# A three-stage kernel on Trainium2: another weight conversion, one form for all experts' second layers, and new planner tables

## The chip, the cores and the metric

The kernel runs on one core of a Trainium2 chip. The metric is the device time of one execution in microseconds, as the median of several runs. Before the change it is 784.63 us (three runs, 784.27 to 784.72).

## What is computed

Three stages, each feeding the next: attention with a hashed mask, a dense two-layer network, and eight experts with a greedy assignment of tokens. All inputs are fp32, except that the network's weights `w_in` and `w_out` come as 64-bit words, of which the kernel reads a high and a low half.

```python
def _attn_ref(q, k, v, proj):            # (2, 8, 768, 64)
    q_bits = (einsum('bhsd,dk->bhsk', q, proj) > 0)    # k likewise
    q_bucket = sum(q_bits * powers)                    # 6 bits
    scores = where(q_bucket == k_bucket, q @ k.T / sqrt(D), -1e9)
    attn = exp(scores - max); attn = attn / (sum(attn) + 1e-9)
    return attn @ v                                    # -> x: 1536 x 512
def _moe_ref(x, w_in, w_out):            # 512 x 2048, 2048 x 512
    h = maximum(x @ w_in, 0)
    return h * h @ w_out
def _moe2_ref(x, w_gate, w1, w2):        # 8 experts, 512 x 1024, 1024 x 512
    order = argsort(-(x @ w_gate).flatten())
    # greedy: each token goes to the first expert in this order that has room (192)
    for e in range(8):
        out[assigned == e] = maximum(x[assigned == e] @ w1[e], 0) @ w2[e]
```

## The kernel before

The program is one core's work on five engines, written in an order that a planner makes. `Sched` holds the operations of each stage: engine, planned duration, what they need, a priority, which buffers they take (`acq`) and give back (`rel`). `order` runs a list schedule with these durations and writes the instructions out in the order that results; `port=True` marks VectorE steps that the planner doesn't let run beside GpSimd's. The tables `PR` (attention), `MP` (network), `EP` and `RP` (router) and `FP` (experts) are priorities by kind of operation. On the chip each engine then works through its own instructions in this order and waits at semaphores; the planner's times decide nothing else.

Attention (0 to about 260 us): 96 blocks of 128 rows. TensorE makes scores (L582), VectorE their maximum (L598), ScalarE the exponential (L601), GpSimd scales (L610), TensorE transposes (L618), ScalarE and VectorE copy the transposes in two parts (L626, L630), TensorE multiplies with the values (L639, L640).

Network (about 240 to 525 us): the weights come in 16 chunks `f`, each an in- and an out-part of 128x512 words. `conv` (L804 to 818) makes fp32 of the two halves: step 0 on ScalarE takes the absolute value of the high half, steps 1 to 4 on VectorE are L812, L814, L816 and L818. `raw` holds the two halves, `t` the word that is put together, `x` the result. Later steps split into fp32r parts (L822, L887, L909), TensorE transposes (L878, L902) and multiplies (L926), and L943 evicts.

Router and experts (525 to 782 us): the router assigns tokens in rounds, on VectorE above all; L1606 are long steps of a round (44 of them, 600 to 1012 ns), L1613 the small matmuls beside them. Each round's end gives the row numbers `ix` of the next expert (L1736). GpSimd fetches these rows by two indirect transfers (L1911), TensorE transposes them (L1929, L1931), and the expert `p` begins: first layer L1967 in four groups `g` of fp32 matmuls, then the second layer. `HP = 2`: experts 0 and 1 take `add2`, the others `add2r`.

- `add2`: after a zeroing matmul (L2014), fp32 matmuls (L2008) give the transposed output, relu'd by ScalarE or VectorE (L1971); it is evicted (L2067 ScalarE, L2069 VectorE), transposed back (L2076), copied (L2083, L2085).
- `add2r`: the second layer's weights are split in two fp32r parts (L1885 ScalarE, L1887 VectorE), the relu'd hidden layer too (L1978 ScalarE, L1981 VectorE, two pieces), and fp32r matmuls of 512 columns give the output itself (L2036, L2037, L2038 for tokens 0 to 127; L2040, L2043 for the rest), evicted at L2099, L2101, L2103.

Then GpSimd scatters the output rows (L2089, L2090), two scatters per expert. All work on GpSimd is in one queue, so a scatter that waits keeps the next gather waiting.

Of the kernel before, what the change touches and what calls it, by code (L numbers as in the profile page):

```python
# [81 lines left out]
class Sched:  # L82
# [24 lines left out]
    def order(self):  # L107
# [51 lines left out]
        while left:  # L159
# [34 lines left out]
            if locks:  # L194
                port = t + dur
# [526 lines left out]
LEAST = 3.4332275390625e-05  # L722
MP = {"lw": -774.5, "ac": 24.5, "h1": -252.5, "h2": 273.5, "ch": -3545, "hw": 253.5, "we": -1093, "wn": -1773, "cv": -742, "sp": -3335.5, "sm": -1005, "xs": -292.5, "sq": -2724, "lg": -93.5, "ev": 307.5, "lv": 292, "c0": 8976.5, "c1": 6037.5, "b0": 230.5, "b1": 3618}


def mlp(nc, S, ps, mem, ident, xhi, xlo, w_in, w_out, w_gate, wgt, x2d, L, att):
# [391 lines left out]
    def last_logits(n, s, rel):  # L1118
# [10 lines left out]
        for h in range(2):  # L1129
            T["lt", n, h] = a = S.add("PE", .22, lambda h=h: half(n, h, 1), [(e, f)[h], a], prio=q, acq=("B",) if h else ("B", "xt"))  # L1130
# [6 lines left out]
    def out(n, s):  # L1137
# [8 lines left out]
        T["lt", n] = a = S.add("PE", .44, lambda: logit(n, 0), [e], prio=p(s, "lg"), acq=["B", "xt"])  # L1146
# [35 lines left out]
    for f in range(16):  # L1182
# [3 lines left out]
        dur = (.61, 1.135, 1.135, 1.14)  # L1186
# [670 lines left out]
def experts(tc, nc, S, ps, mem, ident, router, x2d, w1, w2, out, L, cst, slot):  # L1857
# [43 lines left out]
    def before(p):  # L1901
# [316 lines left out]
```

## Time and profile before

| | |
|---|---|
| median of three runs | 784.63 us |
| profiled execution: its own time | 783.99 us |
| span of its records | 782.2 us |
| TensorE (PE) busy | 755.5 us, 97% |
| VectorE (DVE) busy | 588.1 us, 75% |
| ScalarE (ACT) busy | 462.3 us, 59% |
| GpSimd (POOL) busy | 341.6 us, 44% |

The busy times are sums over instructions on each engine; an fp32 matmul stands in the trace as two records. PEclk is the clock that TensorE was granted, as a share of full speed. Idle time is shown with the instruction that ended it and what it waited for ("<-").

### The profile page before, as it was taken

Reading aid. Unit: us, or ns where it says so; the run is one execution under the profiler, and the core shown is the slowest. Engines: PE = TensorE matmul, PEld = TensorE weight load, DVE = VectorE, ACT = ScalarE, POOL = GpSimd, SP = SyncE. Lnnn points to the kernel's source line nnn. Section 1 sums busy time; section 2 is a strip of 40 time slices with the busy share of each in tenths; the row PEclk is TensorE's granted clock in tenths of the full one; section 3 lists DMA queues with packets and bytes.
Section 4 is the critical chain, followed back from the end, with each engine's and each line's share of the span. In section 5 each row is a group of like instructions: output and inputs, shape, how many; then the busy total and the mean of one; then the engine's idle time right before and its main releaser. Section 6 shows DMA issues by size and latency. Waiting matters only on the chain.

```text
span 782.2 us, 14059 instructions
## 1 busy us (share of the span) xinstructions
PE 755.5 (97%) x4979; PEld 663.1 (85%) x4979; DVE 588.1 (75%) x1243; ACT 462.3 (59%) x949; POOL 341.6 (44%) x376
## 2 busy tenths in 40 slices
PE   8899999999999999999999999999999799999996
PEld 6689888898887889998888989898589698888885
DVE  6789999999999896599979775438877577753432
ACT  7889889889898665553666665455503212333332
POOL 3578788787797776555410000009320412231111
PEclk9999999999999999999999999999799899999999
DMA  8979658575721122310311310201176475897000
GB/s 173 236 139 182 146 108 187 123 136 129 170 60 56 54 74 89 108 54 0 109 54 54 108 55 1 81 27 55 60 252 203 144 259 191 284 340 257 21 12 29
DMA packets 77732, 94.33 MB, mean 121 GB/s; under 512 B 29632, under 2 KB 56640, under 8 KB 77664
## 3 DMA queue, kind: packets, MB, share of 16 engines
q1 hardware_dynamic: 75616, 87.16, 41.1%
q0 software_dynamic: 2048, 6.29, 2.6%
q8 instruction: 39, 0.64, 0.3%
q14 instruction: 29, 0.24, 0.1%
HBM read 63.55 MB, written 6.29 MB: 89 GB/s over the span
## 4 chain that ended last, share of the span: by engine, by line
PE 64%; DVE 17%; issue 9%; ACT 5%; DMA 2%; POOL 1%; SPq 0%; POOLq 0%; ACTq 0%; DVEq 0%
PE psS L926 9%; PE psS L1967 7%; PE psS L582 5%; DVE p L630 4%; PE psTP L902 4%; PE psm L902 4%; DVE f L598 4%; PE psTP L878 3%; PE psO L926 3%; PE psS L2008 2%; PE psTP L926 2%; PE psm L878 2%; DVE tz L865 2%; PE psTP L618 2%; PE psO L1339 1%
## 5 line engine op out<-in xcount | busy, mean ns | idle before, releaser
L610 POOL TENSOR_TENSOR f<-f 128x768 f32<-128x768 f32 x96 | 141.9, 1480 | 30.9 <-PE psTP L618 8.2
L926 PE MATMUL psS<-r 128*128 128x512 f32 x384 | 100.6, 395 | 0.3 <-DVE f L943 0.3
L824 POOL TENSOR_TENSOR r<-f,r 128x384 fp32r<-128x384 f32 (+3 forms) x58 | 74.8, 1312 | 55.6 <-ACT r L822 52.4
L598 DVE TENSOR_REDUCE f<-psS 128x1 f32<-128x768 f32 x96 | 90.7, 946 | 3.6 <-PE psS L582 3.4
L582 PE MATMUL psS<-r 128*128 128x384 f32 x384 | 88.7, 352 | 4.2 <-DMA r<-r 1.8
L601 ACT ACTIVATE f<-psS,f 128x768 f32<-128x768 f32 x96 | 88.1, 917 | 3.4 <-DVE f L598 2.1
L926 PEld LDWEIGHTS psS<-r 128*128 128x128 f32 x384 | 70.5, 188 | 13.6 <-DVE f L943 1.1
L1967 PE MATMUL psS<-ff,rf 128*128 128x192 f32 x400 | 77.8, 338 | 0.0
L582 PEld LDWEIGHTS psS<-r 128*128 128x128 f32 x384 | 64.2, 188 | 10.1 <-ACT f L601 7.1
L822 ACT ACTIVATE r<-f 128x384 fp32r<-128x384 f32 (+3 forms) x112 | 56.4, 533 | 27.7 <-DVE f L818 11.7
L2090 POOL DMA_INDIRECT out_dram<-ff,ix x16 | 22.2, 1385 | 112.1 <-DVE ff L2101 67.2
L1967 PEld LDWEIGHTS psS<-ff,rf 128*128 128x128 f32 x400 | 66.7, 195 | 1.6 <-DVE ff L1938 0.3
L1475 POOL TENSOR_SCALAR f<-f,mx 128x768 bf16<-128x768 f32 (+1 forms) x3 | 8.3, 2755 | 134.5 <-ACT f L1461 134.5
L630 DVE TENSOR_TENSOR p<-psTP,p 128x384 fp32r<-128x384 f32 x93 | 49.8, 548 | 6.4 <-ACT p L626 6.0
L626 ACT ACTIVATE p<-psTP 128x384 fp32r<-128x384 f32 x93 | 45.3, 503 | 8.8 <-PE psTP L618 8.3
L1887 DVE TENSOR_TENSOR ff<-rf,ff 128x1024 fp32r<-128x1024 f32 x22 | 26.9, 1222 | 31.4 <-ACT ff L1885 31.4
L1885 ACT ACTIVATE ff<-rf 128x1024 fp32r<-128x1024 f32 x22 | 23.3, 1058 | 44.6 <-PE psS L2038 36.3
L1911 POOL DMA_INDIRECT ff<-x2d,ix x16 | 19.5, 1218 | 68.8 <-DVE cq L1803 28.8
L618 PE MATMUL psTP<-ident,f 128*128 128x128 f32 x279 | 46.3, 275 | 0.5 <-DVE p L630 0.4
L824 DVE TENSOR_TENSOR r<-f,r 128x384 fp32r<-128x384 f32 (+3 forms) x54 | 30.5, 582 | 18.0 <-ACT r L822 17.9
L913 ACT ACTIVATE f<-f 128x384 f32<-128x384 f32 x63 | 31.9, 521 | 16.2 <-DVE f L909 15.2
L618 PEld LDWEIGHTS psTP<-ident,f 128*128 128x128 f32 x279 | 34.3, 140 | 7.5 <-DVE p L630 2.0
(448 smaller groups left out, 1950.7 us busy)
## 6 DMA issues: line engine op xcount, KB each, us to landing
rf<-in_moe_w_dram SPq DMA_DIRECT2D x60, 512.0 KB, 6.8
r<-r SPq DMA_DIRECT2D x90, 192.0 KB, 4.3
f<-in_moe_w_in_dram SPq DMA_DIRECT2D x16, 512.0 KB, 3.8
f<-in_moe_w_out_dram SPq DMA_DIRECT2D x16, 512.0 KB, 4.7
r<-r SPq DMA_DIRECT2D x15, 384.0 KB, 3.9
f<-in_q_dram SPq DMA_DIRECT2D x8, 384.0 KB, 6.4
f<-in_k_dram SPq DMA_DIRECT2D x8, 384.0 KB, 7.8
f<-in_v_dram SPq DMA_DIRECT2D x8, 384.0 KB, 5.9
```

Of the source, the lines that this page charges most:

```text
L582: nc.tensor.matmul(sbank(u)[:, hf, 0:384], T["q", (pr, h)][:, n, 128 * i:128 * i + 128], T["k", (pr, h)][:, n, 384 * hf:384 * hf + 384], s ...
L598: nc.vector.tensor_reduce(col(0, u), sbank(u)[:, :, 0:384], axis=AX.XY, op=OP.max, negate=True)
L601: nc.scalar.activation(P(u).rearrange("p (a b) -> p a b", a=2), sbank(u)[:, :, 0:384], AF.Exp, bias=col(0, u), accum_out=col(1, u))
L610: nc.gpsimd.tensor_tensor(Pn(u), P(u), col(3, u).to_broadcast([128, 768]), op=OP.mult)
L618: nc.tensor.transpose(tp(u, g)[:, j], Pn(u)[:, 128 * c:128 * c + 128], ident)
L626: nc.scalar.activation(th, tp(u, g), AF.Copy)
L630: nc.vector.tensor_tensor(tl, tp(u, g), th.bitcast(F32), op=OP.subtract)
L822: nc.scalar.activation(hi, x, AF.Copy)
L824: (e or nc.gpsimd).tensor_tensor(lo, x, hi.bitcast(F32), op=OP.subtract)
L902: nc.tensor.matmul(wbank(s, k), w[x][:, c], y[z][:, c], start=st and c == i == 0, stop=c == 1 and i == 2, skip_group_check=not st)
L926: nc.tensor.matmul(abank(i), a[:, t], w, start=(f == RUNS[r][1][0] and j == 0), stop=(f == RUNS[r][1][-1] and j == 2))
L1967: nc.tensor.matmul(abank(n)[:, j], raw(p, g)[:, 0, 256 * c + 128 * j:256 * c + 128 * j + 128], xT(p)[:, c], start=(c == 0), stop=(c == 3))
```

## The change

It has four parts.

- `conv`: ScalarE's absolute value now goes to `t`; a maximum of `t` with the constant `LEAST` (L812, one tensor, in place) replaces the comparison; shift and mask move to L814; the two combining steps stay (L816, L818) and the last writes `x`. The step that multiplied with the comparison's result is gone. Step count stays four on VectorE. `LEAST` gets another value, and the raw buffer is given back with step 4, not 3.
- `HP = 0`: experts 0 and 1 take `add2r` like the others. Buffers `yT` and `hx` go, `wh` gets three places in place of two, `hr` four in place of three, and the raw tiles become 15 in place of 16.
- The planner's durations of GpSimd's transfers (gather 3.6 and 2.1 to 3.8 and 2.7, scatter 1.1 to 1.4) and a weight for the logits' transposes are other numbers; `port` of a VectorE step is tested a little differently.
- All priority tables have new numbers.

From L2033 on, line numbers of the kernel after are two higher.

```diff
-PREP, PW, DL = -40.5, 0.8, 2.4
-PREP1 = 3
+PREP, PW, DL = -38, 0.8, 2.4
+PREP1 = 10
-PR = {"S": 22, "mx": 1264, "ex": -144, ...
+PR = {"S": 21.5, "mx": 2686.5, "ex": 33, ...
-LEAST = 3.4332275390625e-05
+LEAST = 3.0517578125e-05
         if j == 0:
-            nc.scalar.activation(x, hw.bitcast(F32), AF.Abs)
+            nc.scalar.activation(t.bitcast(F32), hw.bitcast(F32), AF.Abs)
         elif j == 1:
-            V.tensor_scalar(t, hw, 3, 0x3FFFFFF8, op0=OP.logical_shift_left, op1=OP.bitwise_and)
+            V.tensor_scalar(t.bitcast(F32), t.bitcast(F32), LEAST, None, op0=OP.max)
         elif j == 2:
+            V.tensor_scalar(t, t, 3, 0x3FFFFFF8, op0=OP.logical_shift_left, op1=OP.bitwise_and)
+        elif j == 3:
             V.scalar_tensor_tensor(t, hw, -0x40000000, t, op0=OP.bitwise_and, op1=OP.bitwise_or)
-        elif j == 3:
-            V.scalar_tensor_tensor(t, lw, 29, t, op0=OP.logical_shift_right, op1=OP.bitwise_or)
         else:
-            V.scalar_tensor_tensor(x, x, LEAST, t.bitcast(F32), op0=OP.is_ge, op1=OP.mult)
+            V.scalar_tensor_tensor(x.bitcast(I32), lw, 29, t, op0=OP.logical_shift_right, op1=OP.bitwise_or)
...
-        dur = (.61, 1.135, 1.135, 1.14)
+        dur = (.61, .61, 1.135, 1.135)
...
-HP = 2
+HP = 0
-RF = (8,) * 11 + (3, 3, 3, 1.5, 1.5)
+RF = (8,) * 11 + (3, 3, 3, 3)
-UNITS_F = {"raw": ..., "wh": (5008, 5016), "yT": (5024, 5027), "yl": (5056,), "hx": (4097, 4098.5, 5030), "hr": (4088, 4091, 4094),
+UNITS_F = {"raw": ..., "wh": (5008, 5016, 5024), "yl": (5056,), "hr": (4088, 4091, 4094, 4097),
...
-        T["ga", p] = ga = S.add("POOL", 2.1 if p else 3.6, gather, [ids], prio=FP["ga"], acq="xg")
+        T["ga", p] = ga = S.add("POOL", 2.7 if p else 3.8, gather, [ids], prio=FP["ga"], acq="xg")
...
+            if (p, g, j, b) == (0, 0, 0, 1):
+                ps.part(unit(("y", p), "S"))
...
-            T["sc"] = a = S.add("POOL", 1.1, lambda h=h: scat(h), [e, T.get("sc")], prio=FP["sc"])
+            T["sc"] = a = S.add("POOL", 1.4, lambda h=h: scat(h), [e, T.get("sc")], prio=FP["sc"])
```

GpSimd's order around the fetch of expert 2, before. `ix_5618` are the row numbers of expert 0, `ix_5961` of expert 1, `ix_6320` of expert 2.

```order
L1911 DMA ff9_5412<-x2d_82,ix_5961 128x512
L1911 DMA ff9_5412<-x2d_82,ix_5961 64x512
L1916 COPY ei_5846<-ei_5846 128x1
L2089 MEMSET pad_93 128x1
L2090 DMA out_0_dram<-ff12_5415,ix_5618 1536x512
L1911 DMA ff8_5411<-x2d_82,ix_6320 128x512
L1911 DMA ff8_5411<-x2d_82,ix_6320 64x512
```

The same place after; the row numbers are `ix_5612`, `ix_5974` and, of expert 2, `ix_6417`.

```order
L1911 DMA ff8_5407<-x2d_82,ix_5974 128x512
L1911 DMA ff8_5407<-x2d_82,ix_5974 64x512
L1916 COPY ei_5842<-ei_5842 128x1
L2091 MEMSET pad_93 128x1
L2092 DMA out_0_dram<-ff11_5410,ix_5612 1536x512
L2091 MEMSET pad_93 128x1
L2092 DMA out_0_dram<-ff12_5411,ix_5612 1536x512
L1911 DMA ff7_5406<-x2d_82,ix_6417 128x512
L1911 DMA ff7_5406<-x2d_82,ix_6417 64x512
```

Before, one scatter of expert 0 stands ahead of the gather of expert 2 and the other behind it; after, both stand ahead.

VectorE around the row numbers of expert 2, before.

```order
L1606 TENSOR_SCALAR ff19_5422<-ff18_5421,mx_6208 128x1152
L2085 COPY ff12_5415<-psO_63 64x512
L1736 CAST ix_6320<-psTP0_60 128x2
L1606 TENSOR_SCALAR ff20_5423<-ff18_5421,mx_6208 128x1152
L1606 TENSOR_SCALAR ff21_5424<-ff18_5421,mx_6208 128x1152
L1606 TENSOR_SCALAR ff22_5425<-ff18_5421,mx_6208 128x1152
L1887 TENSOR_TENSOR ff2_5405<-rf8_5392,ff1_5404 128x1024
```

The same place after.

```order
L1981 SCALAR_TENSOR_TENSOR rf13_5394<-psS10_5435,rf13_5394 128x2x64
L1981 SCALAR_TENSOR_TENSOR rf13_5394<-psS10_5435,rf13_5394 128x2x128
L1718 TENSOR_TENSOR mv_6358<-h_6339,tok1_100 128x9
L1726 TENSOR_TENSOR ff25_5424<-ff30_5429,pk_6349 128x1152
L1720 TENSOR_TENSOR mv_6358<-tok1_100,mv_6358 128x9
L1562 TENSOR_TENSOR Bb_6365<-w_6288,alive1_99 128x72
L1606 TENSOR_SCALAR ff20_5419<-ff17_5416,mx_6270 128x1152
L1564 TENSOR_SCALAR PM_6387<-Bb_6365 128x72
L1606 TENSOR_SCALAR ff21_5420<-ff17_5416,mx_6270 128x1152
L1736 CAST ix_6417<-psm_62 128x2
L1565 TENSOR_TENSOR PM_6387<-PM_6387,mx_6270 128x72
L1887 TENSOR_TENSOR ff6_5405<-rf8_5389,ff5_5404 128x1024
```

The copy of expert 0's output (L2085), whose scatter GpSimd's next row is, stood right ahead of the row numbers; now the steps of the hidden layer's second part (L1981) stand there, and the copy's successor stands 44 rows earlier. After `ix_6417` and the L1887 four L1606 follow in a row; before, seven with an L1887 between them.

## Rows read from the trace of the kernel before

**Rows 1.** Windows: stretch, its length, busy us (and instructions) of each engine, PEclk
```profile
45.00:231.00 186.00, 183.92 (x1199) 163.63 (x1197) 173.94 (x357) 171.57 (x389) 148.29 (x168) 1.00 0.66 139
231.00:395.00 164.00, 157.66 (x825) 140.69 (x826) 140.90 (x197) 96.74 (x197) 102.96 (x91) 1.00 0.20 65
...
565.00:640.00 75.00, 70.89 (x742) 63.95 (x740) 52.19 (x179) 17.39 (x27) 18.25 (x17) 0.94 0.61 202
...
620.00:640.00 20.00, 20.00 (x145) 18.62 (x145) 13.06 (x59) 2.98 (x6) 2.68 (x4) 0.86 0.77 254
```

**Rows 2.** Groups by line and form: engine, operation, shapes, count | busy us, mean ns
```profile
L818 DVE SCALAR_TENSOR_TENSOR f<-f 128x1024 f32<-128x1024 f32 x16 | 21.9, 1370 | 0.3
...
L812 DVE TENSOR_SCALAR f<-f 128x1024 int32<-128x1024 int32 x16 | 12.9, 808 | 1.8 <-DMA f<-in_moe_w_out_dram 1.8
L1606 DVE TENSOR_SCALAR ff<-ff,mx 128x1152 bf16<-128x1152 f32 x16 | 12.2, 811 | 0.7 <-ACT ff L1580 0.7
```

**Rows 3.** Timeline of TensorE, 231 to 395 us, rows with idle time in brackets
```profile
231.05 0.97 PE L582 MATMUL psS<-r 128*128 128x384 f32 x4 [0.32 <-ACT f L601]
...
380.38 1.31 PE L902 MATMUL psTP<-f,r 128*128 128x384 f32 x6 [1.29 <-DVE f L909]
...
394.46 0.72 PE L926 MATMUL psS<-r 128*128 128x512 f32 x2 [0.34 <-DVE f L943]
```

**Rows 4.** Groups by line and form, experts' stage
```profile
L1887 DVE TENSOR_TENSOR ff<-rf,ff 128x1024 fp32r<-128x1024 f32 x22 | 26.9, 1222 | 31.4 <-ACT ff L1885 31.4
...
L2090 POOL DMA_INDIRECT out_dram<-ff,ix x16 | 22.2, 1385 | 112.1 <-DVE ff L2101 67.2 <-DVE ix L1736 22.7 <-DVE m L1560 9.4
...
L1981 DVE SCALAR_TENSOR_TENSOR rf<-psS,rf 128x256 fp32r<-128x256 f32 x18 | 7.4, 414 | 0.0
```

**Rows 5.** Timeline of TensorE, experts: start us, duration us, instruction
```profile
610.56 2.76 PE L2008 MATMUL psS<-rf,rf 128*128 128x192 f32 x16
613.15 1.05 PE L1613 MATMUL psTP<-Bb,ff 128*128 128x8 bf16 x36
...
618.18 0.44 PE L1929 MATMUL psO<-ident,ff 128*128 128x128 f32 x2 [3.55 <-DMA ff<-x2d,ix]
619.18 0.47 PE L1931 MATMUL psO<-ident,ff 64*128 64x64 f32 x2 [0.56 <-DMA ff<-x2d,ix]
...
642.78 0.38 PE L2076 MATMUL psO<-ident,ff 128*128 128x128 f32 x2
...
643.22 0.74 PE L1613 MATMUL psm<-Bb,ff 128*128 128x8 bf16 x24
...
656.94 0.53 PE L2040 MATMUL psS<-ff,rf 128*128 128x512 f32 x1
...
659.40 0.76 PE L1613 MATMUL psO<-Bb,ff 128*128 128x8 bf16 x24
```

**Rows 6.** Timeline of GpSimd: the first gather, one scatter, a later gather
```profile
564.04 1.98 POOL L1911 DMA_INDIRECT ff<-x2d,ix  x1 [11.92 <-ACT ff L1604]
...
608.28 6.21 POOL L2090 DMA_INDIRECT out_dram<-ff,ix  x1 [22.72 <-DVE ix L1736]
614.79 0.97 POOL L1911 DMA_INDIRECT ff<-x2d,ix  x1 [0.31 <-issue]
```

**Rows 7.** Timeline of VectorE in the experts' rounds
```profile
563.00 7.51 DVE L1606 TENSOR_SCALAR ff<-ff,mx 128x1536 bf16<-128x1536 f32 x8
...
571.44 0.17 DVE L1649 TENSOR_SCALAR full<-psm 128x8 f32<-128x8 f32 x1 [0.75 <-PE psm L1613]
...
607.32 0.68 DVE L2085 COPY ff<-psO 64x512 f32<-64x512 f32 x1
607.92 0.14 DVE L1736 CAST ix<-psTP 128x2 int32<-128x2 f32 x1
607.99 2.26 DVE L1606 TENSOR_SCALAR ff<-ff,mx 128x1152 bf16<-128x1152 f32 x3
...
611.31 3.08 DVE L1606 TENSOR_SCALAR ff<-ff,mx 128x1152 bf16<-128x1152 f32 x4
```

More of the change, by code (lines that the diff above doesn't have):

```diff
@@ L149, in when @@
             t = max(free[self.ops[i][0]], ready_at[i])
-            if self.ops[i][11]:
+            if self.ops[i][11] == 1:
                 t = max(t, port)
@@ L194, in order @@
             if locks:
-                port = t + dur
+                port = max(port, t + dur)
             g = self.got[i] = []
@@ L234 @@
 XC = -13
-PREP, PW, DL = -40.5, 0.8, 2.4
-PREP1 = 3
+PREP, PW, DL = -38, 0.8, 2.4
+PREP1 = 10
 LDP = (2, 0)
-PR = {"S": 22, "mx": 1264, "ex": -144, "dn": -3726, "rec": -2216.5, "nrm": 1537.5, "tp": 27.5, "hi": -226, "lo": 175, "pv": 29.5, "oa": -1881.5, "od": -1440.5, "pe": -31.5, "pa": -522, "pd": -2310}
+PR = {"S": 21.5, "mx": 2686.5, "ex": 33, "dn": -4140, "rec": -2506, "nrm": 2825, "tp": 27, "hi": -325, "lo": 490, "pv": 29.5, "oa": -2356.5, "od": -955.5, "pe": -33, "pa": -513.5, "pd": -2541}
 def host_consts_a():
@@ L1129, in last_logits @@
         for h in range(2):
-            T["lt", n, h] = a = S.add("PE", .22, lambda h=h: half(n, h, 1), [(e, f)[h], a], prio=q, acq=("B",) if h else ("B", "xt"))
+            T["lt", n, h] = a = S.add("PE", .22, lambda h=h: half(n, h, 1), [(e, f)[h], a], prio=q, acq=("B",) if h else ("B", "xt"), w=.6)
             d.append(S.add("DVE" if h == 0 else "ACT", .34 if h == 0 else .31, lambda h=h: half(n, h, 2), [a], prio=q, rel=() if h == 0 else [("B", a)]))
@@ L1145, in out @@
         st.append(c)
-        T["lt", n] = a = S.add("PE", .44, lambda: logit(n, 0), [e], prio=p(s, "lg"), acq=["B", "xt"])
+        T["lt", n] = a = S.add("PE", .44, lambda: logit(n, 0), [e], prio=p(s, "lg"), acq=["B", "xt"], w=.6)
         a1 = S.add("ACT", .52, lambda: logit(n, 1), [a], prio=p(s, "lg"))
@@ L1191, in mlp @@
         for j in range(1, 5):
-            a = S.add("DVE", dur[j - 1], lambda f=f, j=j: conv(f, j), [a], prio=p(s, "cv"), port=True, rel={3: [("wr", T["wr", f])], 4: [("wt", T["tm", f])]}.get(j, ()))
+            a = S.add("DVE", dur[j - 1], lambda f=f, j=j: conv(f, j), [a], prio=p(s, "cv"), port=True, rel=[("wr", T["wr", f]), ("wt", T["tm", f])] if j == 4 else ())
         T["cv", f] = a
@@ L1250, in mlp @@
     return [ld[n] for n in range(12)], st, [i for f in range(16) for i in [*Wd[f], *Sd.get(f // 2, [])]], zone_(L1[0])
-EP = {"fr": -277, "lr": -125, "row": -996.5, "col": 1318, "cp": -12, "ca": 817.5, "gp": 1047}
+EP = {"fr": 393.5, "lr": -1345.5, "row": -2192, "col": 1126, "cp": 67, "ca": 828, "gp": 1212}
 CP = (5, 2, 4, 2, 1, 0)
@@ L1260 @@
 ND = 4
-RP = {"fr": 2161.5, "se": -5096.5, "oh": -968.5, "G": 3516, "A": 2902.5, "lr": 1192.5, "pf": -346.5, "id": 443.5, "gp": 2614, "sq": 196, "G1": 1462.5, "A1": -62.5, "ei": -284.5, "up": 1188.5}
+RP = {"fr": 1655.5, "se": -5286, "oh": -123.5, "G": 3612.5, "A": 4057.5, "lr": 1392, "pf": 644, "id": 838.5, "gp": 1659.5, "sq": 151.5, "G1": 1674, "A1": -658.5, "ei": 1159.5, "up": 1373}
 ACT_TILES = {12: (10, 11), 9: (8,), 6: ()}
@@ L1840, in squeeze @@
         st["L"], st["alive"], st["tok"] = a, None, e1
-FP = {"ga": -1074.5, "xp": 2624, "xe": 2280.5, "m1": 2986.5, "re": -1156.5, "m2": 1829, "ye": -1710.5, "yt": 2599.5, "yo": 2225.5, "sc": 1064, "sp": 545, "mr": 2334}
+FP = {"ga": -1206, "xp": 1773.5, "xe": 2674, "m1": 2423, "re": -1200.5, "m2": 1829, "ye": -1710.5, "yt": 2599.5, "yo": 2171, "sc": 1160, "sp": 2026.5, "mr": 2423}
 AP = 5
-HP = 2
+HP = 0
 RSLACK, ESLACK = 0, 0.2
@@ L1848 @@
 SC = 2.2
-RF = (8,) * 11 + (3, 3, 3, 1.5, 1.5)
-FF = (8, 4, 4, 4, 4, 3, 3, 2, 4, 4, 3, 3, 2, 2, 2, 2, 2, 2, 6, 3, 3, 3, 3, 3, 3, 3, 3, 1.25, .75, 2.5, 1.5, 3)
-UNITS_F = {"raw": (*(4000 + 8 * i for i in range(11)), 5000), "wh": (5008, 5016), "yT": (5024, 5027), "yl": (5056,), "hx": (4097, 4098.5, 5030), "hr": (4088, 4091, 4094),
+RF = (8,) * 11 + (3, 3, 3, 3)
+FF = (8, 4, 4, 4, 4, 4, 4, 4, 4, 3, 3, 2, 2, 2, 2, 2, 2, 6, 3, 3, 3, 3, 3, 3, 3, 3, 1.25, .75, 2.5, 1.5, 3)
+UNITS_F = {"raw": (*(4000 + 8 * i for i in range(11)), 5000), "wh": (5008, 5016, 5024), "yl": (5056,), "hr": (4088, 4091, 4094, 4097),
            "xg": (5032, 5036), "xT": (5040, 5043), "yo": (5046, 5048, 5050, 5052, 5054), "A": ()}
```

2 lines of the change are left out of this document (1 added, 1 removed).

## The prediction

> **What bounds the kernel now.** I read the page's share of each engine first, then the busy time of each engine by stage [rows 1], and only then the single instructions of the stages that have idle time. The reader should see three different stages. In the attention (45 to 231 us) TensorE works 183.92 of 186 us, with VectorE at 173.94 and ScalarE at 171.57: three engines are nearly full, and TensorE is the fullest. In the weight conversion and the first half of the first mixture's matmuls (231 to 395) TensorE works 157.66 of 164 us. At the start of the experts (565 to 640) it works 70.89 of 75 us, and here alone the granted clock falls, to 0.86 between 620 and 640 us. So the end is set by TensorE nearly everywhere. A gain must come out of TensorE's own work, out of its 6.3 us of waiting in the second stage, or out of the 4.1 us and the low clock in the third.
>
> **Part 1, the conversion.** Of each of the 16 weight chunks VectorE runs four steps: L812 (808 ns) and the three two-input steps, of which L818, the compare and multiply, takes 1370 ns [rows 2]. The change drops that last step and puts a maximum with one tensor and a constant in its place, in the form of L812. The trace of before has no such maximum in fp32. Nearest rows: L812 at 808 ns with 1024 elements, and L1606, also one tensor and constants, at 811 ns with 1152 elements. I take 0.81 us, so VectorE saves 1370 - 808 = 0.56 us per chunk, 16 x 0.56 = 9.0 us of work. If the maximum ran at the pace of a two-input step, 1.3 us or so, the saving would be about 1 us in all; that is the other bound. ScalarE's absolute value has the same count and shape in both kernels, nothing there.
>
> How much of 9 us of VectorE's work reaches the end? Only what TensorE waits for. Between 231 and 395 us TensorE has 12 gaps, together 6.5 us, the first and the last in [rows 3]; the largest, 1.29 us, waits for VectorE's L909, and nine of the twelve name VectorE. The gaps of ScalarE's L601 (0.32 us in the rows, three such) belong to the last attention blocks and need not go. VectorE's other jobs of that stretch take the freed time first. Value taken: 2 us, bounds 0 (the gaps are set by the retuned order) and 4 (all of VectorE's gaps go). The steps themselves stay in the same place of VectorE's order, with the maximum and the shift where the shift and the first combination stood; what was hidden beside TensorE stays hidden, and the cover is large, since TensorE's work in that stretch doesn't change.
>
> The Trainium skill (VectorE: DVE Perf Modes, section "Mode 2×_2P — use both read ports for one tensor") states that an fp32 step with one tensor can use both read ports for it and give two results a cycle, while a step with two tensors cannot; the two prices of [rows 2], 808 against 1370 ns, agree, and by the rule the maximum would be of the cheap kind, so that the sum would be the 9 us above and not 1.
>
> **Part 2, the second layer of experts 0 and 1.** Before, the two experts have 128 records of L2008 (4 groups each, 8 fp32 matmuls a group, two records a matmul), each of 192 columns; 16 in a row take 613.15 - 610.56 = 2.59 us [rows 5], 0.162 each, so 20.7 us. To these come the 16 records of the output's transposes, L2076: four take 643.22 - 642.78 = 0.44 us [rows 5], so 1.8 us. The zeroing is four short matmuls and stays out. Together 22.5 us. After, 8 groups (two experts of four) take the form that the other six experts have: ten matmuls from 656.94 to 659.40, 2.46 us a group, 19.7 us. TensorE saves 2.8 us. If every one of the ten had the spacing of the later ones in that row, about 0.235, it would be 18.8 us and the zeroing another half, 4.2 saved. I take 3.5.
>
> It costs the other engines. VectorE gets 8 times L1887 (1222 ns) and L1981 (414 ns for the larger of its two pieces, about 0.29 for the smaller, estimated from its half size) [rows 4], 8 x 1.92 = 15.4 us. It loses four relus, two evictions of the transposed output and two copies, and gets two additions, L2101: six steps fewer, the longest of the kind 0.68 us (L2085) [rows 7], so 3 to 4 us. Net about +12 us. ScalarE gets 8 splits of about 1 us; it worked only 17.39 of the 75 us there [rows 1], so they are hidden.
>
> **Part 3, where it falls in the order.** This is the term that I am least sure of, and it is the main one. In before TensorE stops at 614.63 us for 3.55 us, then again for 0.56, because the tokens of expert 2 have not been fetched [rows 5]. The chain behind it: VectorE gives the indices at about 608.0 us (L1736); GpSimd had already been waiting 22.7 us with the scatter of expert 0, which its order puts ahead of the gather and which needs only indices and data that are there at that moment. That scatter takes 6.21 us (all sixteen take 22.2 us [rows 4], so the other fifteen 1.07 each), and only then the gather starts at 614.79 [rows 6]. Beside the scatter VectorE runs seven L1606 and one L1887 without a gap, 607.99 to 614.39 [rows 7]. After the wait TensorE runs slower: the granted clock of 0.86 from 620 to 640 us [rows 1] is 0.14 x 20 = 2.8 us lost. So this place costs 4.1 + 2.8 = 6.9 us.
>
> After the change both scatters of expert 0 stand after earlier rows of VectorE's order, before the indices of expert 2, so GpSimd is free when these come. But the indices come later: from L1649 at 571.44 to L1736, the indices, at 607.92 [rows 7] VectorE has 103 instructions in before, 124 in after: seven more L1887 (8.6 us), fourteen pieces of L1981 (4.9), three more L1606 (2.4), less two relus and one eviction (1.7): +14.2 us. By the mean durations of their lines the 103 sum to 31.8 us and took 36.5, so 4.7 us were waiting. After: 45.8 us of work, with between none and all of that waiting, so indices at 617.2 to 621.9 us. The two fetches and their landing took 614.49 to 619.18, 4.7 us, in before, which gives data at 621.9 to 626.6.
>
> When does TensorE want them? Before the transposes for expert 2 it has 83 fp32 matmuls of expert work in before (two records of 0.162 us each, 83 x 0.324 = 26.9 us), in after 64 of these and 72 in the new form, 64 x 0.324 + 72 x 0.246 = 38.4 us. So it arrives 11.5 us later than 614.63, at 626.1 us. The data is there 4.2 us early, or 0.5 late. The stall then goes for the most part, and with it the low clock. What is late next is VectorE's chain itself, with hardly a microsecond to spare. Ceiling: 3.5 + 6.9 = 10.4 us; I take 8 and leave 2.4 for waits at the same or the next expert. After that TensorE is dense until the last expert, and the tail after its last matmul is unchanged.
>
> **Part 4, the retuned tables and GpSimd's planned durations.** The first 33 us of TensorE's order are the same. In the attention the softmax blocks' transposes stand about 0.3 us of matmuls further behind their scores than before, and the period of a block is the same. Nothing of TensorE's work changes. I take 0, bounds -1 and +1.
>
> **Sum.** The profiled execution took 783.99 us, 0.64 below the median of 784.63. 783.99 - 2 - 8 = 774.0; with the 0.64 the forecast is 774.5. Its own range is 770 to 779.
>
> **The rivals.**
> A: GpSimd is starved again, or VectorE's chain is the bound. In after the gather of expert 2 stands beside L1887 and four L1606 (4.5 us), as the scatter stood beside seven and took 6.21 us. Against it: the gather of expert 0 ran 1.98 us beside a burst of 7.51 us of L1606 [rows 6, 7]. If it takes 5 us more, data comes at 626.9 to 631.6, TensorE waits 1 to 6 us and the clock falls again: most of 6.9 us stays. Then 784.63 - 3.5 - 1 = 780, between 778.5 and 783.5. The Trainium skill (SBUF — State Buffer, section "Who interferes with whom") states that VectorE in a two-port step and GpSimd shut each other out for the whole instruction, and that descriptor generation is starved so; the scatter's 6.21 us agrees, the first gather's 1.98 us does not in full.
> B: the change does nothing that can be seen. VectorE's saving is hidden in the first mixture, and the wait at expert 2 comes back as waiting for the later indices: 784.6 - 0 to 1.5. For it: VectorE is the busiest after TensorE in all stages.
> C: slower. The retuned table of the attention leaves TensorE waiting at the softmax blocks. There are 96 blocks; with VectorE at 94% and ScalarE at 92% of that stage [rows 1] there is little slack. At 0.2 us a block, the size of the gaps at 231 us [rows 3], it is 19 us, so 774.5 + 19 = 793; from 0.1 us a block on the kernel is slower than before. Against it: in the present order such gaps come only at the end of the stage, and the lag behind the scores got longer, not shorter.
> D: all waits go, 10.4 us in the experts and 4 in the conversion, with the median offset: 784.63 - 14.4 = 770, down to 767 with the upper saving of part 2 and one us in the attention.
>
> **Chances.** Forecast 0.50, A 0.22, B 0.08, C 0.10, D 0.10. Within 0.2% is within 1.6 us of 784.63, about what a measurement of this kernel can tell from no change. Faster 0.82, same 0.08, slower 0.10. The range goes from 766.5 to 783.5: it takes in the forecast, A and D, and leaves B and C out.
>
> **What would show it.** L812 and L814 each near 0.8 us and no compare step, VectorE 9 us less busy between 231 and 480 us, and fewer gaps on L887 and L909: part 1. No L2008 and L2076, L2040's line (two further down) at 64 records: part 2. The gather of expert 2 taking about 1 us, TensorE's wait there under 2 us, and a granted clock near 1.0 from 620 to 640: part 3. I am wrong if a gap of over 5 us stands at expert 2 or 3, or if TensorE's busy share between 45 and 231 us falls under 97%.

## The result and the profile after

The changed kernel takes **777.36 us** (four runs, 775.61 to 777.99) against 784.67 us of the kernel before in the same comparison: a ratio of 0.9901, with a 95% interval from 0.9881 to 0.9921. The forecast was 774.5 us, the range 766.5 to 783.5. Direction and range hold; the gain is 7.3 us where 10.1 was forecast, and the terms are further off than their sum, since errors of both signs cancel in part.

The profiled execution of the changed kernel took 777.99 us, its span is 776.2 us. Its windows answer to [rows 1] (stretch, length, busy us of PE, PEld, DVE, ACT, POOL, then the granted clock):

```profile
45.00:231.00 186.00, 183.20 (x1185) 161.22 (x1184) 171.05 (x352) 170.91 (x382) 145.01 (x167) 1.00 0.64 138
231.00:395.00 164.00, 157.93 (x835) 140.77 (x834) 133.28 (x200) 98.64 (x203) 100.79 (x94) 1.00 0.19 65
...
565.00:640.00 75.00, 73.50 (x777) 60.04 (x776) 63.71 (x192) 34.55 (x46) 16.11 (x17) 1.00 0.57 191
```

At the start of the experts VectorE works 63.71 of 75 us, 11.5 more than before, TensorE waits less (73.50 busy against 70.89), and the clock stays at full speed. In the two earlier stages nothing has got better: TensorE's 183.20 and 157.93 us stand against 183.92 and 157.66.

How the 6.0 us of span divide is best read from where stages begin and end on TensorE. Below are one line's records with the times of the first and the last start, first of the kernel before (L640 is the attention's last kind of matmul, L902 the last transposes of the network, L1967 the experts' first layer, L2038 the last matmul of all):

```profile
L640 PE MATMUL psm<-p x30: 334/338/423, 64.3 to 272.7; 128*128 128x384 f32 x30
...
L902 PE MATMUL psTP<-f,r x84: 331/334/441, 380.4 to 519.3; 128*128 128x384 f32 x84
...
L1967 PE MATMUL psS<-ff,rf x400: 323/326/662, 571.9 to 767.2; 128*128 128x192 f32 x134
...
L2038 PE MATMUL psS<-ff,rf x48: 387/392/398, 650.9 to 775.5; 128*128 128x512 f32 x48
```

and of the changed kernel (L2040 is its L2038):

```profile
L640 PE MATMUL psTP<-p x42: 331/338/347, 78.4 to 276.9; 128*128 128x384 f32 x42
...
L902 PE MATMUL psTP<-f,r x162: 331/335/446, 383.9 to 523.7; 128*128 128x384 f32 x162
...
L1967 PE MATMUL psS<-ff,rf x400: 323/326/431, 577.1 to 760.1; 128*128 128x192 f32 x134
...
L2040 PE MATMUL psS<-ff,rf x64: 388/393/398, 583.9 to 769.5; 128*128 128x512 f32 x64
```

| TensorE's stage | before | after | change | forecast |
|---|---|---|---|---|
| start to the last L640 | 272.7 | 276.9 | +4.2 | 0 |
| to the last L902 (network) | 246.6 | 246.8 | +0.2 | -2 |
| to the first L1967 (router) | 52.6 | 53.4 | +0.8 | 0 |
| to the last matmul (experts) | 203.6 | 192.4 | -11.2 | -8 |
| to the end of the span | 6.7 | 6.7 | 0 | 0 |

The conversion's steps, answering to [rows 2], cost what was worked out. L812 is now the maximum, L814 the shift:

```profile
L816 DVE SCALAR_TENSOR_TENSOR f<-f 128x1024 int32<-128x1024 int32 x16 | 20.8, 1298 | 0.2
...
L818 DVE SCALAR_TENSOR_TENSOR f<-f 128x1024 int32<-128x1024 int32 x16 | 20.2, 1263 | 0.1
...
L812 DVE TENSOR_SCALAR f<-f 128x1024 f32<-128x1024 f32 x16 | 13.4, 836 | 13.8 <-ACT f L810 13.8
L814 DVE TENSOR_SCALAR f<-f 128x1024 int32<-128x1024 int32 x16 | 13.3, 830 | 0.2
```

836 and 830 ns for the two cheap steps, and no compare: VectorE has 214.7 us of work between 231 and 525 us, where the same order with the old steps has 224.0 (run e6 below), 9.3 us. None of it is seen in the network's 246.8 us. The first of the four steps now reads what ScalarE's L810 writes, and VectorE stands idle for it for 13.8 us in all, where the shift of before waited 1.8.

TensorE's idle rows between 231 and 395 us, answering to [rows 3]; the first and the last two of ten:

```profile
234.80 0.52 PE L618 MATMUL psm<-ident,f 128*128 128x128 f32 x3 [0.42 <-DVE p L630]
...
368.64 1.31 PE L878 MATMUL psTP<-r,f 128*128 128x384 f32 x6 [0.69 <-DVE f L887]
...
392.58 1.34 PE L902 MATMUL psTP<-f,r 128*128 128x384 f32 x6 [0.85 <-DVE f L909]
```

VectorE still ends the waits (L887, L909), at other places, 5.9 us in all ten against 6.5 in twelve.

At expert 2, GpSimd's and TensorE's rows answer to [rows 5] and [rows 6]. First GpSimd:

```profile
610.14 0.94 POOL L2092 DMA_INDIRECT out_dram<-ff,ix  x1 [14.12 <-DVE Z L1651]
...
612.54 1.41 POOL L2092 DMA_INDIRECT out_dram<-ff,ix  x1 [1.35 <-ACT ff L2101]
624.10 1.86 POOL L1911 DMA_INDIRECT ff<-x2d,ix  x1 [10.16 <-DVE PM L1565]
```

Both scatters of expert 0 are gone at 614 us, and the gather starts at 624.10, 0.4 us after VectorE's L1736 at 623.67 (the bracket names the step behind that, L1565). Then TensorE:

```profile
630.45 0.40 PE L2045 MATMUL psS<-ff,rf 128*64 128x512 f32 x1
630.69 0.28 PE L1658 MATMUL psTP<-ident,X 128*8 128x128 f32 x1
630.80 0.38 PE L1929 MATMUL psTP<-ident,ff 128*128 128x128 f32 x2
631.11 0.34 PE L1931 MATMUL psTP<-ident,ff 64*128 64x64 f32 x2
```

No bracket stands in these rows: the transposes of expert 2 wait for nothing.

### The profile page after: what moved, and what is told of

Its sections match the earlier page's. It is cut to its first block, busy times and chain, and to the rows that moved or that the text cites. A ratio compares the mean times of both kernels' runs of the same rounds, so it can differ in the third digit from the quotient of the medians.

```text
span 776.2 us, 13942 instructions
## 1 busy us (share of the span) xinstructions
PE 751.1 (97%) x4906; PEld 649.2 (84%) x4906; DVE 587.4 (76%) x1261; ACT 477.3 (61%) x961; POOL 336.1 (43%) x376
## 4 chain that ended last, share of the span: by engine, by line
PE 60%; DVE 13%; issue 10%; ACT 8%; DMA 4%; POOL 3%; SPq 0%; POOLq 0%; ACTq 0%; DVEq 0%
PE psTP L902 8%; PE psS L926 8%; PE psS L1967 7%; PE psS L582 5%; PE psTP L878 3%; PE psTP L618 3%; PE psm L926 2%; PE psO L926 2%; ACT p L626 2%; DVE f L598 2%; DVE tz L865 2%; DVE p L630 2%; ACT f L601 2%; PE psm L618 1%; DMA f<-in_moe_w_out_dram 1%
## 5 line engine op out<-in xcount | busy, mean ns | idle before, releaser
L824 POOL TENSOR_TENSOR r<-f,r 128x384 fp32r<-128x384 f32 (+3 forms) x58 | 71.9, 1262 | 59.5 <-ACT r L822 58.2
L582 PE MATMUL psS<-r 128*128 128x384 f32 x384 | 89.7, 355 | 2.4 <-DMA r<-r 2.0
L1967 PE MATMUL psS<-ff,rf 128*128 128x192 f32 x400 | 75.6, 332 | 0.0
L582 PEld LDWEIGHTS psS<-r 128*128 128x128 f32 x384 | 66.1, 191 | 7.3 <-ACT f L601 4.1
L1967 PEld LDWEIGHTS psS<-ff,rf 128*128 128x128 f32 x400 | 65.2, 190 | 2.3 <-DVE ff L1938 0.3
L630 DVE TENSOR_TENSOR p<-psTP,p 128x384 fp32r<-128x384 f32 x104 | 56.2, 547 | 6.9 <-ACT p L626 5.8
L2092 POOL DMA_INDIRECT out_dram<-ff,ix x16 | 17.1, 1071 | 101.1 <-DVE ff L2103 54.5
L1885 ACT ACTIVATE ff<-rf 128x1024 fp32r<-128x1024 f32 x30 | 31.7, 1056 | 46.5 <-PE psS L2040 36.4
L878 PE MATMUL psTP<-r 128*128 128x384 f32 x312 | 57.1, 337 | 1.9 <-DVE f L887 1.9
L878 PEld LDWEIGHTS psTP<-r 128*128 128x128 f32 x312 | 54.4, 188 | 3.8 <-DVE f L887 3.2
L1887 DVE TENSOR_TENSOR ff<-rf,ff 128x1024 fp32r<-128x1024 f32 x30 | 36.7, 1222 | 23.5 <-ACT ff L1885 22.3
L618 PE MATMUL psTP<-ident,f 128*128 128x128 f32 x312 | 51.7, 274 | 2.0 <-ACT r L501 0.9
L626 ACT ACTIVATE p<-psTP 128x384 fp32r<-128x384 f32 x104 | 50.6, 494 | 3.2 <-PE psTP L618 2.0
L618 PEld LDWEIGHTS psTP<-ident,f 128*128 128x128 f32 x312 | 38.7, 140 | 10.8 <-issue 4.7
```

Of the source, the lines that this page charges most:

```text
L582: nc.tensor.matmul(sbank(u)[:, hf, 0:384], T["q", (pr, h)][:, n, 128 * i:128 * i + 128], T["k", (pr, h)][:, n, 384 * hf:384 * hf + 384], s ...
L618: nc.tensor.transpose(tp(u, g)[:, j], Pn(u)[:, 128 * c:128 * c + 128], ident)
L626: nc.scalar.activation(th, tp(u, g), AF.Copy)
L630: nc.vector.tensor_tensor(tl, tp(u, g), th.bitcast(F32), op=OP.subtract)
L824: (e or nc.gpsimd).tensor_tensor(lo, x, hi.bitcast(F32), op=OP.subtract)
L878: nc.tensor.matmul(hbank(s, hf), w[:, c % 2], y[:, x, sl], start=(c == 0 and i == 0), stop=(c == 3 and i == 2))
```

## The experiments

Each kernel's ratio is to the kernel before, run on the same chip in the same job; medians of different jobs differ by up to 1.5 us for the same kernel, so ratios are compared, and us only by stages of the traces.

**e1: the conversion's steps alone.** The kernel before, in its own order on every engine:

```diff
-            nc.scalar.activation(x, hw.bitcast(F32), AF.Abs)
+            nc.scalar.activation(t.bitcast(F32), hw.bitcast(F32), AF.Abs)
...
+            V.tensor_scalar(t.bitcast(F32), t.bitcast(F32), LEAST, None, op0=OP.max)
...
-            V.scalar_tensor_tensor(x, x, LEAST, t.bitcast(F32), op0=OP.is_ge, op1=OP.mult)
+            V.scalar_tensor_tensor(x.bitcast(I32), lw, 29, t, op0=OP.logical_shift_right, op1=OP.bitwise_or)
```

> The kernel before, in its own order on every engine; only the conversion's four VectorE steps and ScalarE's first step take the new form. Theory 1 (the saving is hidden: in the changed kernel TensorE's waits between 231 and 395 us sum to 6.07 us against 6.34 before): VectorE 8 to 9 us less busy, TensorE's end moves by 0 to -1 us, 784 to 785. Rival (the prediction's part 1): TensorE's nine gaps on VectorE shrink, 2 to 4 us faster, 781 to 782.5.

830.02 us, ratio 1.0563 [1.0539, 1.0587]: both theories fell, and the reason is the experiment's own. The low half `lw` is now read in step 4, but the order still gave the raw buffer back with step 3, so a later chunk's load stood ahead of that step. VectorE's waits (line, what it waited for, us in total, times, longest):

```profile
DVE f L818 <- DMA f<-in_moe_w_out_dram: 50.9, 11, 5.5
```

Eleven of the sixteen last steps waited for a load. Their own chunk's had long landed, since the steps before them read it; so by the order it was another chunk's, whose low bits they took. The run says nothing on what the steps are worth; it says that the change's small line on the buffer's release is a needed part, and that an order which is right in form can cost 45 us here.

**e5: the conversion with its release and its planned durations.** As e1, and

```diff
-        dur = (.61, 1.135, 1.135, 1.14)
+        dur = (.61, .61, 1.135, 1.135)
-... rel={3: [("wr", T["wr", f])], 4: [("wt", T["tm", f])]}.get(j, ()))
+... rel=[("wr", T["wr", f]), ("wt", T["tm", f])] if j == 4 else ())
```

> As the run of the conversion alone, but with what that run had left out: the raw buffer is given back with step 4, where its low half is now last read (there the next chunk's load stood ahead of that step, so it waited for the load and took the low bits of another chunk), and the planner has the new durations, so it writes another order. Everything else as before. Theory 1 (TensorE's work covers VectorE's saving): 783 to 785. Rival (part 1 of the prediction): 781 to 782.5. Third (the first step on VectorE now has to wait for ScalarE's, which it didn't before, and this delays the conversion wherever tables weren't made for it): 787 or more.

787.33 us, 1.0029 [1.0013, 1.0045]: 2 us slower, between theory 1 and the third. In its trace the network takes 247.6 us on TensorE and the experts 204.5, about 1 us more each, and the attention, from the first L640 to the last, 240.7 against 239.7. The conversion by itself, in an order that the old tables give, is no gain.

**e6: the reverse, the old steps in the changed kernel's order.** Every engine keeps the changed kernel's order; only `conv` and `LEAST` are those of before.

> The changed kernel in its own order on every engine, with the conversion's old steps (compare and multiply; the absolute value beside them). VectorE gets 7 to 9 us more work between 231 and 480 us. Theory 1 (hidden): within 1 us of the changed kernel, 776 to 778.5. Rival (in this order the saved VectorE time is used): 3 us or more slower, 780 to 783.

778.07 us, 0.9911 [0.9887, 0.9935], against 0.9901 of the changed kernel: theory 1. Its windows:

```profile
231.00:395.00 164.00, 156.96 (x830) 140.02 (x829) 139.17 (x198) 98.29 (x202) 105.54 (x94) 1.00 0.19 65
395.00:525.00 130.00, 129.74 (x670) 116.74 (x669) 84.83 (x139) 77.49 (x151) 2.42 (x1) 1.00 0.15 53
```

VectorE has 139.17 and 84.83 us here, 133.28 and 81.46 with the new steps, and TensorE is busy the same (286.7 against 287.7 of 294 us). So 9.3 us of VectorE's work are worth less than the measurement can tell.

**e2: the second layers alone.** The kernel before with

```diff
-HP = 2
+HP = 0
```

and the changed kernel's buffers; all tables as before.

> The kernel before with both second layers of experts 0 and 1 in two fp32r parts (its buffers with it), all tables, durations and the conversion as before. Theory 1 (the form of the second layer and the two scatters that move ahead of the third gather give the experts' gain, the tables don't): 8 to 11 us faster, 774 to 776.5, no wait of over 2 us at expert 2 and no fall of the clock at 620 us. Rival (the new tables and durations of GpSimd's transfers make the stall go): 3 us of TensorE's work only, 781 to 782, with a wait of 3 us or more at expert 2 or 3.

780.61 us, 0.9931 [0.9909, 0.9954], nearer the rival's time, but without its wait. In the trace the experts take 200.9 us from the first L1967 to the last matmul, 2.8 less than before (the profiled execution took 782.14 us, 1.5 more than the median). The scatters move ahead as foreseen and the transposes of expert 2 don't wait. But small waits of TensorE come up elsewhere; from the first L1967 on they sum to 5.5 us, where the kernel before has 5.0 and the changed kernel 0.9. The longest is

```profile
696.15 0.27 PE L1658 MATMUL psTP<-ident,X 128*8 128x128 f32 x1 [1.44 <-DVE X L1653]
```

and the clock in the stretch from 620 to 640 us is 0.91:

```profile
620.00:640.00 20.00, 18.03 (x181) 15.24 (x180) 15.25 (x45) 7.29 (x10) 5.11 (x7) 0.91 0.59 205
```

So the form gives TensorE's work back, and the stall's place is free, but in this trace the stage keeps most of its lost time until the order fits.

**e7: the experts' old table in the changed kernel.**

```diff
-FP = {"ga": -1206, "xp": 1773.5, "xe": 2674, "m1": 2423, ...
+FP = {"ga": -1074.5, "xp": 2624, "xe": 2280.5, "m1": 2986.5, ...
```

> The changed kernel with the old table of priorities of the experts, FP. From the first expert matmul to the last, TensorE takes 203.6 us in the kernel before, 200.9 with the new second layer alone and 192.4 in the changed kernel; the new layer alone thus gives 3 of 11 us. Theory 1 (the rest comes from the order in the experts): 4 us slower or more than the changed kernel, 781 to 786, with the clock's fall back in the experts. Rival (it comes from the router's tables or the planned durations of GpSimd): within 1.5 us of the changed kernel, 776 to 779.

782.62 us, 0.9971 [0.9953, 0.999]: theory 1, some 5 us slower than the changed kernel. The experts take 196.6 us, 4.2 more than there. The clock's fall that theory 1 asked for is small (0.98 between 565 and 640 us, against 1.00). The largest of TensorE's waits is 1.85 us, in a router round:

```profile
584.45 0.17 PE L1404 MATMUL psTP<-mm,tri 128*128 128x24 bf16 x1 [1.85 <-DVE mm L1682]
```

**e9: the router's old tables in the changed kernel.** `EP` and `RP` as before.

> The changed kernel with the router's two old tables, EP and RP. The new second layer alone gave 4.3 us, the experts' old table in the changed kernel cost 5.3. Theory 1 (the router's rounds on VectorE are part of the same chain, so their table matters as much): 780 to 784, with TensorE's waits at an expert's transposes or a fall of the clock. Rival (the experts' table alone does it): 776 to 779.

840.04 us, 1.0682 [1.0649, 1.0714]: theory 1, and far past its numbers. The windows:

```profile
620.00:640.00 20.00, 17.73 (x153) 15.28 (x152) 6.79 (x12) 4.12 (x7) 3.46 (x6) 0.95 0.13 40
640.00:660.00 20.00, 11.94 (x165) 9.55 (x162) 15.94 (x54) 5.33 (x7) 2.78 (x3) 0.50 0.40 130
...
680.00:700.00 20.00, 20.00 (x108) 17.77 (x107) 7.90 (x15) 6.61 (x10) 2.38 (x4) 1.00 0.34 118
700.00:720.00 20.00, 11.11 (x132) 8.28 (x130) 13.14 (x53) 3.44 (x6) 5.92 (x6) 0.74 0.26 85
```

From 640 to 660 us TensorE works 11.94 of 20 us at half clock. Until 656.9 us it has no expert's work and follows the round on VectorE step by step: it waits 4.0 us in all for L1606, 2.0 for L1557, 1.0 for L1653. The same repeats from 704 us on. These two tables, together with the rest of the order, set whether a round stands beside an expert's matmuls or behind them.

**e8: the planner's old durations of GpSimd's transfers.**

```diff
-        T["ga", p] = ga = S.add("POOL", 2.7 if p else 3.8, gather, ...
+        T["ga", p] = ga = S.add("POOL", 2.1 if p else 3.6, gather, ...
-            T["sc"] = a = S.add("POOL", 1.4, ...
+            T["sc"] = a = S.add("POOL", 1.1, ...
```

> The changed kernel with the planner's old durations of GpSimd's gathers and scatters; all tables new. Theory 1 (the planned durations place the gathers' users later, so that TensorE doesn't stop at them): TensorE waits 2 us or more at the transposes of an expert, the clock falls there, 780 to 785. Rival (a few tenths in the plan change nothing that lasts): 776 to 779.

776.39 us, 0.9902 [0.9874, 0.9929], the same as the changed kernel: the rival. The new durations in the plan move rows of the order and nothing of the time that these runs can tell.

**e4: is GpSimd starved, or is it its queue?** The kernel before; GpSimd's first scatter of expert 0 behind the gather of expert 2:

```diff
+        seq.remove(self.late[0])
+        seq.insert(seq.index(self.late[1]) + 1, self.late[0])
```

> The kernel before with one change of order on GpSimd: the first scatter of expert 0 stands behind the gather of expert 2, not ahead of it. Theory 1 (the prediction's rival A: whatever GpSimd issues at 608 us is starved beside seven L1606 in a row): the gather takes the 6 us in the scatter's place, its data comes 2 to 3 us earlier at most, TensorE still waits 1.5 us or more: 781.5 to 784. Theory 2 (it is the queue's order): the gather takes 1 to 2 us at 608.3, the data is there at 612 to 613, TensorE's 4.1 us of waiting and the fall of the clock go: 777.5 to 779.

783.47 us, 0.9974 [0.9962, 0.9985]: theory 1. The gather takes the scatter's place and its 6 us (line numbers here are some lines higher; L1917 is the gather, L2096 the scatter, L1609 the long step):

```profile
609.95 6.17 POOL L1917 DMA_INDIRECT ff<-x2d,ix  x1 [22.80 <-DVE ix L1739]
...
617.64 0.93 POOL L2096 DMA_INDIRECT out_dram<-ff,ix  x1 [0.19 <-issue]
...
609.60 2.26 DVE L1609 TENSOR_SCALAR ff<-ff,mx 128x1152 bf16<-128x1152 f32 x3
...
612.92 3.07 DVE L1609 TENSOR_SCALAR ff<-ff,mx 128x1152 bf16<-128x1152 f32 x4
```

It ends at 616.1, when VectorE's L1609 end (612.92 + 3.07 = 615.99), as the scatter did in the kernel before. TensorE's transposes still wait:

```profile
618.63 0.44 PE L1935 MATMUL psO<-ident,ff 128*128 128x128 f32 x2 [2.39 <-DMA ff<-x2d,ix]
```

2.4 us in place of 3.6. Freeing the queue alone is worth 2 us. That the rest goes with the meeting with VectorE's long steps is argued from these rows; no run took away the meeting alone.

**e3: the attention's old table and start numbers in the changed kernel.**

```diff
-PREP, PW, DL = -38, 0.8, 2.4
-PREP1 = 10
-PR = {"S": 21.5, "mx": 2686.5, ...
+PREP, PW, DL = -40.5, 0.8, 2.4
+PREP1 = 3
+PR = {"S": 22, "mx": 1264, ...
```

> The changed kernel with the attention's old table and its two old start numbers. In the trace of the changed kernel the attention's last matmul stands 4.1 us later than before. Theory 1 (the new table of the attention costs that): 773 to 774, the attention's last matmul back at 272 to 273 us. Rival (the 4 us are what the router and the later stages need anyway, or are given back there: the experts wait for the router, not for the attention): 776.5 to 778.

774.61 us, 0.986 [0.9836, 0.9885], near theory 1's time: 2.8 us faster than the changed kernel by the medians, 3.6 by the spans of the traces. Its place is reached only in part: the last L640 starts at 275.1, not at 272 to 273, and the first L1967 at 573.6, against 276.9 and 577.1 in the changed kernel. So 1.8 us of the trace's 3.6 come in the attention; from the last L902 to the first L1967 it is 51.3 us against 53.4, and why that is so these runs leave open. The experts take 192.3 us, as there (192.4).

**e10: only the start numbers of e3**, `PREP` and `PREP1`.

> The changed kernel with the attention's two old start numbers and its new table PR. Both old gave 774.6. Theory 1 (the loss lies in the first 45 us: in the trace the attention is 1.2 to 3.7 us behind there, the clock falls once at 29 us): 774 to 775.5. Rival (the steady part's drift, 0.45 us per 30 us, is the table PR's, and the start is no matter): 776.5 to 778.

776.4 us, 0.9875 [0.9848, 0.9903]. By the median it lies at 776, between; in its trace the last L640 starts at 277.1, as late as in the changed kernel, and from the first L640 to the last it takes 244.3 us, more than the changed kernel's 242.6. So the loss is not in the start: the rival, though the time alone doesn't settle it.

**e11: the experts' part alone.** The kernel before with the new second layers and `FP`, `EP`, `RP`; attention, network, conversion and planned durations as before.

> The kernel before with the new second layers and the new tables of router and experts; attention, network, conversion and the planned transfer times as before. Theory 1 (the whole gain lies in the experts, and the conversion gives nothing that reaches the end): 773 to 775.5. Rival (the conversion and its table are needed for it): 777 or more.

775.02 us, 0.9843 [0.9814, 0.9872]: theory 1. Its interval lies below that of the changed kernel. The network takes 246.6 us in its trace, with the old conversion.

**e12: the changed kernel less the two parts that cost or give nothing** (old attention table, old planned durations).

> The changed kernel with the attention's old table and start numbers and with the planner's old durations of the transfers, the two parts that cost something or nothing by themselves. Theory 1 (the two add up): 773 to 774.5, faster than both kernels. Rival (the planner's order depends on all numbers together, so that the sum doesn't hold): 775 or more.

775.23 us, 0.9864 [0.9838, 0.989]: no faster than e3 or e11, the rival. All three have lower ratios than the changed kernel's 0.9901; only e11's interval lies wholly below its interval, and the runs don't tell the three apart.

## Why the prediction was right, and where it was wrong

**Second layer of experts 0 and 1** (forecast -3.5). Right. From each matmul's start to the next, the old form's three lines (L2008, L2014, L2076) take 23.8 us in the trace of before. The new form's five lines take 58.3 us there for six experts, and for eight 79.4 in the changed kernel and 77.9 in e2: 21.1 and 19.6 us for the two experts, so 2.7 and 4.2 us saved, the two values between which 3.5 was taken.

**The stall at expert 2** (forecast -4.5 of a possible 6.9, mechanism). Right in place and times. The stage begins 5.2 us later than before (577.1 against 571.9). The indices were forecast for 617.2 to 621.9, and they come at 623.67, so at 618.5 on the old scale. TensorE's arrival was forecast for 626.1; it comes at 630.80, so 625.6. No wait is left, and the clock doesn't fall. Two terms were mis-sized. Of the 2.4 us left for waits "at the same or the next expert" only one wait of 0.86 us is there, in a router round at 589.0 us. And the fall of the clock cost more than the 2.8 us counted from 620 us on: it begins before, with 0.97 between 600 and 620 us, another 0.6 us. With it the ceiling is 11.0 in place of 10.4, and the experts gain 11.2. Where I read this from the changed kernel's order without asking which part of the change makes that order, e2, e7 and e9 tell: the second layer's form without the new tables gives 0.7% and not 1.6, the old `FP` takes 5 us away, the old `EP` and `RP` 60. The experts' and router's tables, which my part 4 put at nothing, carry more than half of the gain of e11 (12.3 us by its ratio, of which e2 has 5.4). The prices don't add up: the 60 us of e9 are those of an order mixed from old and new tables, not the worth of the new ones.

**The conversion** (forecast -2). Wrong. The 9.0 us of VectorE's work were right, 9.3 measured. The step that failed is the choice of 2 us out of TensorE's 6.5 us of waiting. The network takes 246.6 us on TensorE in the kernel before, in e2 and in e11 (old steps), 246.8 in the changed kernel (new steps): it is TensorE's work and a few waits whose sum the planner's order sets, not the speed of the step that ends them. The bound of 0 that I wrote down was the value.

**The attention** (forecast 0, bounds -1 and 1). Wrong by 4.2 us, outside the bounds. It has two parts. The first L640 starts at 33.1 us before and at 34.3 after. TensorE's order up to there is the same in all kernels, and their traces have this start anywhere from 32.1 (e2) to 34.6 us (e7), so these 1.2 us can't be put down to the change. What is seen in the changed kernel's trace is a lower granted clock between 28 and 36 us; e11, whose attention has the order of before, has it too, and its first L640 starts at 34.2 (the rows are of before, the changed kernel and e11):

```profile
28.00:36.00 8.00, 6.18 (x38) 5.05 (x39) 4.30 (x9) 4.80 (x11) 2.45 (x3) 1.00 1.03 239
...
28.00:36.00 8.00, 6.55 (x30) 5.00 (x31) 3.44 (x6) 3.30 (x7) 1.76 (x2) 0.79 1.03 235
...
28.00:36.00 8.00, 6.56 (x30) 5.00 (x31) 3.62 (x6) 3.31 (x7) 1.80 (x2) 0.79 1.05 235
```

The other 3.0 us are the order's, still outside the bounds. From the first L640 to the last the kernel before takes 239.7 us, and e2, e4 and e11, with its order, 239.7 to 240.0; the changed kernel takes 242.6, and e6 to e9, with its order, 242.6 to 243.6; e3 and e12, with the old table and the new conversion, take 240.5 to 240.7, as e5 does. So about 2 us come with the attention's table and 1 with the conversion. In the times, too, the old table is worth about 3 us: ratios of 0.986 in e3 and e12 against 0.990 to 0.991 in the changed kernel, e6 and e8. The failed sentence is "Nothing of TensorE's work changes". The same matmuls take longer when they stand in another row. The value matmul L639, by its mean (ns), before:

```profile
L639 PE MATMUL psTP<-p,r 128*128 128x384 f32 x60 | 23.2, 386 | 0.1
...
L639 PE MATMUL psTP<-p 128*128 128x384 f32 x48 | 18.6, 388 | 0.0
```

and after:

```profile
L639 PE MATMUL psTP<-p,r 128*128 128x384 f32 x48 | 18.8, 393 | 0.1
...
L639 PE MATMUL psTP<-p 128*128 128x384 f32 x42 | 16.8, 401 | 0.0
```

The timeline of the kernel before shows why one L639 differs from another:

```profile
103.01 0.34 PE L640 MATMUL psm<-p,r 128*128 128x384 f32 x1
103.19 0.33 PE L639 MATMUL psm<-p,r 128*128 128x384 f32 x1
103.36 0.34 PE L640 MATMUL psm<-p,r 128*128 128x384 f32 x1
103.54 0.49 PE L618 MATMUL psTP<-ident,f 128*128 128x128 f32 x3
103.79 0.42 PE L639 MATMUL psm<-p,r 128*128 128x384 f32 x1
104.05 0.34 PE L640 MATMUL psm<-p,r 128*128 128x384 f32 x1
```

L639 behind L640 is followed by the next matmul after 0.17 us (103.19 to 103.36), L639 behind three short transposes after 0.26 (103.79 to 104.05). L639 behind transposes is found 95 times of 192 before, 123 times in the changed kernel, 99 in e3 and 95 in e11. But the other matmuls of 384 columns pay for this place too: L582 has 0.27 us behind transposes and 0.18 behind another L582, and it stands there 30 times in place of 45. All of 384 columns together stand behind transposes 165 times before and 173 after, and what they take there beyond 0.175 us sums to 13.9 and 15.1 us. That is 1.2 of the 3.0 us. TensorE's idle time in the attention grew by 0.7 us (4.6 to 5.3 from the first L640 on). About 1 us isn't located, and none of the experiments changed the neighbours alone. e10 speaks against them as the main cause: it has 164 such places with 14.2 us, and its attention takes longest of all. So it is shown that the order costs time there, and open by what. The lag that I had looked at, from scores to transposes, says whether data is late, and nothing else of an order.

**Smaller slips of the prediction.** Its sum, 774.0 and 0.64, gives 774.6, and rival D's lower end comes to about 768.5 by its own terms, not 767. "Here alone the granted clock falls" holds for the three stretches named there, not for the kernel: between 540 and 560 us it is 0.74 before and 0.71 after.

**The rivals.** A, that GpSimd is starved beside VectorE's long steps: the 6 us are seen again (e4: 6.17 us), but in the changed kernel the gather of expert 2 takes 1.86 us. B: it holds for the conversion and not for the experts. C named the attention as the place of a loss, with waits at the softmax blocks as its mechanism. The place was right, at 0.03 us per block; of the mechanism only the 0.7 us of idle time. D asked for all waits gone: the experts came near that, the conversion didn't, and the attention's order took 3 us back.

## What to carry to other kernels

Work that a helper engine saves counts only where the full engine waits in sum, not where a wait carries the helper's name; swap the old step back into the new order to see it. Where a change carries new numbers for a planner, cost the order apart from the instructions: an order can lose time on the fullest engine with not one instruction more. Before a stage is compared between two traces, look at the granted clock in it. And parts that come together should be run apart before all are kept: here the conversion, which saves 9 us of an engine's work, was worth nothing, and one table took back about a quarter of the gain.

## What the runs showed of the hardware

An indirect transfer of GpSimd that started inside a row of VectorE's long one-tensor steps took 6.21 and 6.17 us, to the end of that row; the first gather of the kernel before, also inside such a row (eight steps), took 1.98 us; one that started beside L1887, a step of two tensors, took 1.86 us though four of the long steps followed it, and the next, wholly beside those four, 1.14 us:

```profile
626.27 1.14 POOL L1911 DMA_INDIRECT ff<-x2d,ix  x1 [0.30 <-issue]
...
623.88 1.22 DVE L1887 TENSOR_TENSOR ff<-rf,ff 128x1024 fp32r<-128x1024 f32 x1
625.02 3.01 DVE L1606 TENSOR_SCALAR ff<-ff,mx 128x1152 bf16<-128x1152 f32 x4
```

So a meeting with these steps isn't always starvation; what decides it these runs leave open. The Trainium skill (SBUF — State Buffer, section "Who interferes with whom") says that VectorE in a two-port step and GpSimd shut each other out for a whole instruction, and that the one that issues first has the ports: the 6.2 us agree, the 1.14 and 1.98 us beside such steps don't. The second point is the price of a neighbour on TensorE: a matmul of 384 columns behind three transposes of 128 takes 0.09 us more to its successor than one behind another of 384 columns, with no idle time in the record (L639 0.26 against 0.17 us, L582 0.27 against 0.18 in the mean). The third is that the clock can fall in one execution and not in another with the same TensorE order: 0.79 between 28 and 36 us in e11, 1.00 in e2, after nearly the same work (TensorE busy 6.24 and 6.21 of the 8 us before).
